# Token-set parts split when made and loaded straight into place, and a second place for raw gate and up weights, in a spectral-plus-gated kernel

## The chip, the cores and the metric

One core of one Trainium2 chip. The metric is device microseconds for one execution of the kernel. The program uses TensorE (PE, with its weight loads PEld), VectorE (DVE), ScalarE (ACT), GpSimd (POOL, here mostly issuing DMAs) and SyncE (SP, which issues the other DMAs). The engines run side by side and meet at semaphores; each works through its own instructions in order.

## The reference

```python
def reference(A_x, A_dft_seq_re, A_dft_seq_im, A_dft_hid_re, A_dft_hid_im, B_x, B_W_gate, B_W_up, B_W_down):
    xn = _layernorm(A_x, axis=-1)                 # x is [1, 2048, 640]
    # _A_ref: Re(DFT_seq(DFT_hid(xn)))
    a = jnp.einsum("bsd,ed->bse", xn, dft_hid_re)
    b = jnp.einsum("bsd,ed->bse", xn, dft_hid_im)
    y = jnp.einsum("ts,bse->bte", dft_seq_re, a) - jnp.einsum("ts,bse->bte", dft_seq_im, b)
    # _B_ref: gated ReLU unit, F = 1728
    gate = jnp.einsum("bsd,df->bsf", xn, W_gate)
    up = jnp.einsum("bsd,df->bsf", xn, W_up)
    h = gate * (gate > 0) * up
    return A_x + y + jnp.einsum("bsf,fd->bsd", h, W_down)
```

All tensors are float32. The three gated weights are scaled by 64.

## The kernel before

**Products.** Every float32 operand is held as two parts, a high part (the value rounded for TensorE, copied by ACT in `split`, L123) and a low part (value minus high, a DVE subtraction, L124). A product is three matmuls, high by high, high by low, low by high (`mm3`, L129 to L131), each 128x128 by 128x512. The matrix products are arranged in the manner of Strassen, so sums and differences of blocks are made on DVE first.

**Phase 1: the sequence transform, up to about 404 us.** Four chunks of 512 output columns. The matrices come in blocks of 128x1024 (512 KB) by SP (`stream`, L593, loads at L599) into `raw` and `tk` tiles, DVE takes differences (L595), `split` writes both parts into one of three `cb` tiles, and PE uses them against the normalized tokens (`xs_late`, `xs_early`). A list of units (`todo`) is walked by `drive` (L677): each unit's load is issued four units ahead, its preparation two ahead, its matmuls now. Deferred work is put into the same walk at a later unit by `defer(units, f)`. `phase` (L697) writes the list from names: `T1` to `T4` and `B22` are blocks of the transform, `K` and `A` loads of token sets. Within phase 1 a scheduler then orders the instructions of each engine; in phase 2 PE, DVE and ACT keep the program's order.

**Token sets.** The gated unit works on two pairs of token blocks, 1024 tokens each. Each pair has nine blocks of 128x1024: B11 to B22, T1 to T4 and X4. For the first pair (index 1) they are made in phase 1 by `token_sets` (L320), in six steps put into the list nine units apart. A step loads raw rows and statistics into two `stage` tiles by POOL (L362, L363), makes normalized blocks (L368, L369) and differences (L375) on DVE six units later, and stores them to DRAM (`set1`) by POOL two units after that (L384): one block half in each of steps 0 and 1, four halves as two stores of 512 KB in each of steps 2 to 5. In the last chunk `load_set` (L661) brings each whole block back by SP to a `stage` tile (L669) and splits it with ACT and DVE into its place: the four T sets (`K`) into `r1`, the other five (`A`) into `xs_early`. The second pair's sets are made and brought back in phase 2 with the same functions.

**Phase 2: gate and up, after about 404 us.** `gate_up(n)` (L786) makes one unit of 128 gated features against the sets of a pair. `Weights` (L744) loads raw gate and up blocks to the tile `z` (SP, L750), makes sums on DVE (L756 to L760), and splits them into `gw` with ACT copies through L120 and subtractions (L770). The pool of `z` has one place; `Weights(n+2)` is created in `rest_ahead` of unit n. ACT also copies PSUM results (`p<-ps` and others, through L120). The remaining 64 features have a unit of their own (`gate_up_rest`, L858, rectifier L872). Phase 3 (`project`) does the hidden transform and the down projection.

Of the kernel before, what the change touches and what calls it, by code (L numbers as in the profile page):

```python
# [58 lines left out]
def fnet_reglu_kernel(  # L59
# [15 lines left out]
    nc = tc.nc  # L75
    keep = ctx.enter_context(tc.tile_pool(name="keep", bufs=1))
# [3 lines left out]
    dram_p = ctx.enter_context(tc.tile_pool(name="dram", bufs=1, space=bass.MemoryType.DRAM))  # L80
# [8 lines left out]
    xs_early = early_p.tile([P, D * S // P], F32R, name="xs_early")  # L89
# [1 line left out]
    eps_t = keep.tile([P, 1], F32, name="eps_t")  # L91
    stat = keep.tile([P, 2, NG, SG], F32, name="stat")
    rows = dram_p.tile([2, S], F32, name="rows")
    sets = [dram_p.tile([NSET, P, W2], F32, name=f"set{q}") for q in range(2)]

    firsts = [dram_p.tile([P, 3, CH], F32, name=f"first{c}") for c in range(NCHUNK)]
    pqd = [dram_p.tile([2, P, KD, CH], F32, name=f"pq{c}") for c in range(NCHUNK)]
# [18 lines left out]
    def stage():  # L116
        return stages[-1].tile([P, W2], F32, name="st")
# [4 lines left out]
    def split(hi, lo, src):  # L122
        nc.scalar.activation(hi, src, AF.Copy)  # L123
        return nc.vector.tensor_tensor(lo, src, hi.bitcast(F32), op=OP.subtract)  # L124
# [30 lines left out]
    ph1 = ExitStack()  # L155
# [2 lines left out]
    tk = ph1.enter_context(tc.tile_pool(name="tk", bufs=NH))  # L158
    sums = ph1.enter_context(tc.tile_pool(name="sums", bufs=1))
    small = ph1.enter_context(tc.tile_pool(name="small", bufs=2))  # L160
    late_p = ph1.enter_context(tc.tile_pool(name="late", bufs=1, side="right"))
    xs_late = late_p.tile([P, D * S // P], F32R, name="xs_late")

# [19 lines left out]
    late = {}  # L183
# [136 lines left out]
    def token_sets(q, step, stage=stage, unit=None):  # L320

        ch = xt[:, q * W2 : (q + 1) * W2].rearrange("(k p) t -> k p t", p=P)
        st_r = rows[:, q * W2 : (q + 1) * W2]
        tt = nc.vector.tensor_tensor
        part = lambda st, i: st[:, i * CH : (i + 1) * CH]
        t = {}

        def later(load, make, keep):
            def begin():
                load()  # L330
                for m in make:
                    defer(6, m)
                defer(8, keep)

            todo.append((begin, idle, idle, idle))

        unit = unit or later

        if step < 2:
            cs = slice(step * CH, (step + 1) * CH)  # L340

            def load():
                t["mr"], t["a"] = stage(), stage()[:, :CH]
                for i in range(2):
                    nc.gpsimd.dma_start(part(t["mr"], i), st_r[i : i + 1, cs].to_broadcast([P, CH]))
                nc.gpsimd.dma_start(t["a"], ch[4][:, cs])

            def make():
                tc.keep_in_program_order(tt(t["a"], t["a"], part(t["mr"], 0), op=OP.add))
                tt(t["a"], t["a"], part(t["mr"], 1), op=OP.mult)  # L350

            unit(load, [make], lambda: nc.gpsimd.dma_start(sets[q][X4][:, cs], t["a"]))
            return

        k, hs = (step - 2) // 2, (step - 2) % 2 * HC
        hs = slice(hs, hs + HC)
        cols = lambda ap: ap.rearrange("p (c t) -> p c t", c=2)

        def load():
            t["mr"], t["ab"] = stage(), stage()  # L360
            for i in range(2):
                nc.gpsimd.dma_start(cols(part(t["mr"], i)), cols(st_r[i : i + 1])[:, :, hs].to_broadcast([P, 2, HC]))  # L362
                nc.gpsimd.dma_start(cols(part(t["ab"], i)), cols(ch[k + 2 * i])[:, :, hs])  # L363

        def make():
            mr, ab = t["mr"], t["ab"]
            for i in range(2):
                tc.keep_in_program_order(tt(part(ab, i), part(ab, i), part(mr, 0), op=OP.add))  # L368
                tt(part(ab, i), part(ab, i), part(mr, 1), op=OP.mult)  # L369

        def more():

            mr, ab = t["mr"], t["ab"]
            (a0, a1, b0, b1), (t1, t2, t3, t4) = ([st[:, i * HC : (i + 1) * HC] for i in range(4)] for st in (ab, mr))
            sub = lambda o, i0, i1: tt(o, i0, i1, op=OP.subtract)  # L375
            sub(t1, a1, a0)
            sub(t2, b1, t1)
            sub(t3, b1, a1)
            sub(t4, b0, t2)

        def keep_sets():
            cs = slice(k * CH + hs.start, k * CH + hs.stop)
            for i, st in ((B11, t["ab"]), (T1, t["mr"])):
                nc.gpsimd.dma_start(sets[q][i : i + 4, :, cs].rearrange("i p t -> p i t"),  # L384
                                  st.rearrange("p (i t) -> p i t", i=4))

        unit(load, [make, more], keep_sets)

    def raw():
        return raw_p.tile([P, W2], F32, name="raw")  # L390
# [202 lines left out]
    def stream(c, name, g):  # L593
# [53 lines left out]

        todo.append((load, prepare, run, lambda: combine(c, name) if g == NH - 1 else None))

    def set_parts(q, i):  # L650
        if i in SETS_A:
            t, b = xs_early, (SETS_A_NEXT, SETS_A)[q].index(i) * 2 * W2
        else:
            t, b = late["sets_b"][q], SETS_B.index(i) * 2 * W2
        return t[:, b : b + W2], t[:, b + W2 : b + 2 * W2]

    def set_half(q, i, j):
        h, l = set_parts(q, i)
        return h[:, j * CH : (j + 1) * CH], l[:, j * CH : (j + 1) * CH]

    def load_set(q, blocks, get=stage):  # L661
        t = {}

        def load():
            if "sets_b" not in late:
                late["sets_b"] = {1: get_r1(F32R)}
            for i in blocks:
                t[i] = get()
                nc.sync.dma_start(t[i], sets[q][i])  # L669

        def prepare():
            for i in blocks:
                split(*set_parts(q, i), t[i])

        return load, prepare, idle, idle

    def drive(far, ahead):  # L677

# [18 lines left out]
    def phase(c, names):  # L697


        for n in names.split():  # L700
            if n == "K":
                todo.append(load_set(1, [first_sets.pop(0)]))
            elif n == "A":
                todo.append(load_set(1, [early_sets.pop(0)]))
            elif n[0] == "W":
                sums_124(int(n[1]))
            elif n[0] == "V":
                sums_3(int(n[1]))
            elif n[0] == "B" and n[2] == "1":
                first_stream(int(n[3]), n[:3], int(n[4]))  # L710
            else:
                stream(c, n[:-1], int(n[-1]))
            if n == "V3":
                free[0] = len(todo) + 2
            if free[0] is not None and len(todo) >= free[0] and steps:
                token_sets(*steps.pop(0))
                free[0] = len(todo) + SPACE
# [6 lines left out]
    for c in range(1, NCHUNK - 1):  # L724
        phase(c, "T10 T11 T12 T13 T20 B220 T21 B221 T22 T23 B222 B223 T30 T31 T32 T33 T40 T41 T42 T43")
    assert not steps, len(steps)
    phase(NCHUNK - 1, "T10 K T11 T12 K T13 T20 B220 K T21 B221 K T22 T23 B222 B223 T30 A T31 A T32 A T33 A T40 A T41 T42 T43")
    assert not early_sets and not first_sets
    drive(4, 2)
    ph1.close()  # L730


    ph2 = ExitStack()
    for n, b, side in (("prep", 2, "left"), ("z", 1, "left"), ("wr", 1, "left"), ("tmp", 1, "left"), ("hob", 2, "left"),
                       ("stage3", 2, "left"), ("sets", 1, "left"), ("gw1", 1, "right")):
        open_pools[n] = ph2.enter_context(tc.tile_pool(name=n, bufs=b, side=side, reuse_waits="tile"))
    pool = open_pools.__getitem__
# [48 lines left out]
    def gate_up(n):  # L786
# [110 lines left out]

    def next_set(i, n, since=1, get=stage3, soon=False):

        load, prepare, _, _ = load_set(0, [i], get)  # L900

        def first():
            if 0 not in late["sets_b"] and i in SETS_B:
                late["sets_b"][0] = pool("sets").tile([P, len(SETS_B) * 2 * W2], F32R, name="sets_b")
            load()

        loads[n - since].append(first)
        (urgent if soon else besides)[n].append(prepare)

    def pair_weights(k, n):  # L910

# [338 lines left out]
```

## Time and profile before

| | |
|---|---|
| Median of three timed runs | 1047.72 us (1043.9 to 1048.57) |
| Profiled execution, first to last instruction (span) | 1043.3 us; no other time of this execution is recorded |
| Mean granted TensorE clock in it | 0.997 |
| TensorE busy | 1028.4 us |
| VectorE busy | 802.1 us |
| ScalarE busy | 433.5 us |
| GpSimd busy | 95.7 us |
| DMA | 233.29 MB, mean 224 GB/s |

How to read what follows. The windows view gives, for each stretch, the busy time of every engine with its number of instructions, the granted clock (1.00 is full), the DMA share and GB/s. The waits view lists, for an engine, which group waited for which, the total, the number and the longest. The chain follows the work that ended last backwards; a row is start, length, what. The timeline's rows are start, length, engine, line, operation, output and input, count, and in brackets the idle time ahead with what released it. Buffer numbers are left out of names, so `st` is any `stage` tile and `cb` any of three. Successive matmuls overlap, so their pitch is read from their starts.

### The profile page before, as it was taken

The numbers are of one execution on the slowest core, as the hardware profiler recorded it, in microseconds if no ns is written. First come the engines' busy times: TensorE is split into PE (matmuls) and PEld (weight loads), VectorE is DVE, ScalarE is ACT, GpSimd is POOL, SyncE is SP. The second block draws the span as 40 slices with busy tenths as digits, with TensorE's granted clock in tenths as the row PEclk, the third lists the DMA queues.
The fourth block names the chain that finished last, engine by engine and source line by source line (L and its number), as shares of the span: only waits on it lengthen the run. The fifth ranks groups of instructions, "written<-read, shape, count | busy, mean of one in ns | idle before, by whom it ended". The sixth has DMA issues, their size and how long they took to land.

```text
span 1043.3 us, 12416 instructions
## 1 busy us (share of the span) xinstructions
PE 1028.4 (99%) x4528; PEld 847.3 (81%) x4528; DVE 802.1 (77%) x1071; ACT 433.5 (42%) x543; POOL 95.7 (9%) x156
## 2 busy tenths in 40 slices
PE   8999999999999899899999999999999999999998
PEld 7888888888887788688888888888888888888886
DVE  7857886978979887577887988887488667786764
ACT  6654453333333443333334534343355423552521
POOL 2000010101211001421110000100000000000000
PEclk9999999999999999999999999999999999999999
DMA  7985754958867863863364566565498637986454
GB/s 294 340 247 170 261 161 140 311 205 269 305 199 259 339 203 116 251 222 143 131 206 177 203 224 232 215 237 188 145 393 287 207 111 218 366 300 233 157 159 121
DMA packets 100156, 233.29 MB, mean 224 GB/s; under 512 B 11392, under 2 KB 50816, under 8 KB 98688
## 3 DMA queue, kind: packets, MB, share of 16 engines
q1 hardware_dynamic: 83664, 166.96, 47.6%
q0 software_dynamic: 16432, 65.55, 17.4%
q8 instruction: 35, 0.57, 0.2%
q14 instruction: 25, 0.20, 0.1%
HBM read 177.41 MB, written 54.02 MB: 222 GB/s over the span
## 4 chain that ended last, share of the span: by engine, by line
PE 84%; DMA 5%; DVE 5%; issue 4%; ACT 2%; POOL 0%; SPq 0%; ACTq 0%; POOLq 0%; DVEq 0%
PE ps L131 27%; PE ps L130 27%; PE ps L129 27%; DMA z<-in_wgu 2%; DVE cb L124 1%; DMA r<-in_x 1%; DMA st<-set 1%; PE ps L1147 1%; PE ps L483 1%; ACT cb L123 1%; DMA set<-st 1%; DMA rw<-hd 1%; DVE raw L595 0%; DVE gw L770 0%; ACT gw L120 0%
## 5 line engine op out<-in xcount | busy, mean ns | idle before, releaser
L131 PE MATMUL ps<-cb,wt 128*128 128x512 f32 x390 | 151.9, 390 | 0.1
L129 PE MATMUL ps<-cb,wt 128*128 128x512 f32 x390 | 151.8, 389 | 0.0
L130 PE MATMUL ps<-cb,wt 128*128 128x512 f32 x390 | 151.7, 389 | 0.0
L124 DVE TENSOR_TENSOR cb<-rw,cb 128x1024 fp32r<-128x1024 f32 x83 | 94.2, 1135 | 66.6 <-ACT cb L123 65.9
L123 ACT ACTIVATE cb<-rw 128x1024 fp32r<-128x1024 f32 x83 | 81.9, 987 | 145.2 <-PE ps L131 125.0
L123 ACT ACTIVATE cb<-raw 128x1024 fp32r<-128x1024 f32 x78 | 82.5, 1059 | 124.9 <-PE ps L131 108.3
L124 DVE TENSOR_TENSOR cb<-raw,cb 128x1024 fp32r<-128x1024 f32 x78 | 95.1, 1221 | 41.2 <-ACT cb L123 38.0
L130 PE MATMUL ps<-xs_early,gw 128*128 128x512 f32 x260 | 101.2, 389 | 0.0
L129 PE MATMUL ps<-xs_early,gw 128*128 128x512 f32 x260 | 101.2, 389 | 0.0
L131 PE MATMUL ps<-xs_early,gw 128*128 128x512 f32 x260 | 101.1, 389 | 0.0
L130 PE MATMUL ps<-cb,xs_late 128*128 128x512 f32 x256 | 99.8, 390 | 0.9 <-DVE cb L124 0.8
L131 PE MATMUL ps<-cb,xs_late 128*128 128x512 f32 x256 | 99.7, 389 | 0.3 <-DVE xs_late L251 0.3
L129 PE MATMUL ps<-cb,xs_late 128*128 128x512 f32 x256 | 99.6, 390 | 0.4 <-ACT cb L123 0.4
L130 PE MATMUL ps<-cb,xs_early 128*128 128x512 f32 x238 | 92.8, 390 | 1.5 <-DVE cb L124 1.5
L129 PE MATMUL ps<-cb,xs_early 128*128 128x512 f32 x238 | 92.6, 391 | 1.1 <-ACT cb L123 1.1
L120 ACT ACTIVATE gw<-z 128x1024 fp32r<-128x1024 f32 (+1 forms) x52 | 57.8, 1111 | 84.2 <-DVE z L760 68.7
L131 PE MATMUL ps<-cb,xs_early 128*128 128x512 f32 x238 | 92.1, 389 | 0.0
L131 PEld LDWEIGHTS ps<-cb,wt 128*128 128x128 f32 x390 | 73.2, 188 | 15.7 <-DVE wt L124 0.5
L130 PEld LDWEIGHTS ps<-cb,wt 128*128 128x128 f32 x390 | 73.2, 188 | 15.4
L129 PEld LDWEIGHTS ps<-cb,wt 128*128 128x128 f32 x390 | 73.2, 188 | 15.2
L120 ACT ACTIVATE u<-ps 128x512 f32<-128x512 f32 x52 | 31.2, 599 | 93.0 <-PE ps L131 93.0
L770 DVE TENSOR_TENSOR gw<-z,gw 128x1024 fp32r<-128x1024 f32 (+1 forms) x52 | 64.8, 1286 | 2.3 <-ACT gw L120 2.2
(192 smaller groups left out, 1932.1 us busy)
## 6 DMA issues: line engine op xcount, KB each, us to landing
raw<-in_dft SPq DMA_DIRECT2D x94, 512.0 KB, 5.7
wt<-wparts SPq DMA_DIRECT2D x66, 256.0 KB, 3.2
z<-in_wgu SPq DMA_DIRECT2D x26, 640.0 KB, 4.0
hd<-ob POOLq DMA_DIRECT2D x26, 512.0 KB, 3.5
rw<-hd SPq DMA_DIRECT2D x24, 512.0 KB, 6.1
wparts<-pw POOLq DMA_DIRECT2D x11, 1024.0 KB, 4.1
tk<-in_dft SPq DMA_DIRECT2D x16, 512.0 KB, 6.2
rw<-pq SPq DMA_DIRECT2D x16, 512.0 KB, 7.7
```

The source lines that it names most:

```text
L120: return nc.scalar.activation(o, i, AF.Copy)
L123: nc.scalar.activation(hi, src, AF.Copy)
L124: return nc.vector.tensor_tensor(lo, src, hi.bitcast(F32), op=OP.subtract)
L129: nc.tensor.matmul(ps, wh, mh, start=first, stop=False, skip_group_check=more)
L130: nc.tensor.matmul(ps, wh, ml, start=False, stop=False, skip_group_check=more)
L131: nc.tensor.matmul(ps, wl, mh, start=False, stop=last, skip_group_check=more)
L483: nc.tensor.matmul(E[c, key], xn_part(j, d)[v == 1], b[c][0][:, int(v == 2), j], start=j == 0 and v == 0, stop=False)
L770: tt(self.w[:, 1, cs], self.z[:, cs], self.w[:, 0, cs].bitcast(F32), op=OP.subtract)
L1147: nc.tensor.matmul(B[key], wr[:, v, es], hr[:, cs], start=False, stop=v == 1, skip_group_check=not new)
```

## The change

Three parts. (1) The first pair's sets become `halves`, with a high and a low part of each block in DRAM. In each of its steps, `halve` splits a finished tile: the high part by ACT to a new tile `hi` (a pool of one place, shared by both tiles of a step), the low part by DVE in place of the block; `keep` stores the two parts by POOL. The first tile of a step is split six units after the loads and stored one later, the second two units after the first. (2) In the last chunk `load_halves` brings both parts of a block by one SP DMA of 1 MB straight to their place, with no stage tile and no split; the `K` loads stand later in the list, the `A` loads begin earlier. (3) The pool of `z` has two places, `Weights(n+2)` is created at the beginning of `gate_up(n)`, and the pools of phase 2 are opened in another order. In the new file the sources of `split` are at L124 and L125, matmuls at L130 to L132, DFT loads at L617 and their differences at L613, high and low stores at L399 and L400, `load_halves` at L687.

```diff
-    sets = [dram_p.tile([NSET, P, W2], F32, name=f"set{q}") for q in range(2)]
+    sets = dram_p.tile([NSET, P, W2], F32, name="set0")
+    halves = dram_p.tile([NSET, P, 2, W2], F32, name="set1")
...
+    high_p = ph1.enter_context(tc.tile_pool(name="high", bufs=1))
...
-        def later(load, make, keep):
-            def begin():
-                load()
-                for m in make:
-                    defer(6, m)
-                defer(8, keep)
-
-            todo.append((begin, idle, idle, idle))
...
+            made = [([make, more], "ab", lambda v: halves[B11 : B11 + 4, :, v, cs].rearrange("i p t -> p i t"), by_set),
+                    ([], "mr", lambda v: halves[T1 : T1 + 4, :, v, cs].rearrange("i p t -> p i t"), by_set)]
...
+        def begin():
+            load()
+            for i, (make, name, place, view) in enumerate(made):
+
+                def halve(make=make, name=name):
+                    for m in make:
+                        m()
+                    src = t[name]
+                    if "h" not in t:
+                        t["h"] = high_p.tile([P, W2], F32R, name="hi")
+                    split(t["h"][:, : src.shape[1]], src.bitcast(F32R), src)
+
+                def keep(name=name, place=place, view=view):
+                    src = t[name]
+                    nc.gpsimd.dma_start(place(0), view(t["h"][:, : src.shape[1]].bitcast(F32)))
+                    nc.gpsimd.dma_start(place(1), view(src))
+
+                defer(6 + 2 * i, halve)
+                defer(7 + 2 * i, keep)
+
+        todo.append((begin, idle, idle, idle))
...
-    def load_set(q, blocks, get=stage):
-        t = {}
+    def load_halves(i):
 
         def load():
             if "sets_b" not in late:
                 late["sets_b"] = {1: get_r1(F32R)}
-            for i in blocks:
-                t[i] = get()
-                nc.sync.dma_start(t[i], sets[q][i])
-
-        def prepare():
-            for i in blocks:
-                split(*set_parts(q, i), t[i])
-
-        return load, prepare, idle, idle
+            t, b = set_place(1, i)
+            nc.sync.dma_start(t[:, b : b + 2 * W2].bitcast(F32), halves[i].rearrange("p v t -> p (v t)"))
+
+        todo.append((load, idle, idle, idle))
...
-    phase(NCHUNK - 1, "T10 K T11 T12 K T13 T20 B220 K T21 B221 K T22 T23 B222 B223 T30 A T31 A T32 A T33 A T40 A T41 T42 T43")
+    phase(NCHUNK - 1, "T10 T11 T12 T13 T20 K B220 K T21 K B221 K T22 A T23 A B222 B223 T30 A T31 A T32 A T33 T40 T41 T42 T43")
...
-    for n, b, side in (("prep", 2, "left"), ("z", 1, "left"), ("wr", 1, "left"), ("tmp", 1, "left"), ("hob", 2, "left"),
+    for n, b, side in (("prep", 2, "left"), ("tmp", 1, "left"), ("wr", 1, "left"), ("hob", 2, "left"), ("z", 2, "left"),
                        ("stage3", 2, "left"), ("sets", 1, "left"), ("gw1", 1, "right")):
...
+        if n + 2 < NU:
+            weights[n + 2] = Weights(n + 2)
         for f in issues[n]:
             f()
...
-            if n + 2 < NU:
-                weights[n + 2] = Weights(n + 2)
             for f in loads[n]:
                 f()
```

The second pair keeps whole blocks: it takes the same functions through `unit`, `keep_whole` and `next_set`, which now has the load and the split written out.

More of the change, by code (lines that the diff above doesn't have):

```diff
@@ L326, in token_sets @@
         t = {}
-        def later(load, make, keep):
-            def begin():
-                load()
-                for m in make:
-                    defer(6, m)
-                defer(8, keep)
-            todo.append((begin, idle, idle, idle))
-        unit = unit or later
         if step < 2:
@@ L350, in make @@
                 tt(t["a"], t["a"], part(t["mr"], 1), op=OP.mult)
-            unit(load, [make], lambda: nc.gpsimd.dma_start(sets[q][X4][:, cs], t["a"]))
-            return
[L355 to L387, printed above, removed]
+            made = [([make], "a", lambda v: halves[X4][:, v, cs], lambda ap: ap)]
+            keep_whole = lambda: nc.gpsimd.dma_start(sets[X4][:, cs], t["a"])
+        else:
+            k, hs = (step - 2) // 2, (step - 2) % 2 * HC
+            hs = slice(hs, hs + HC)
+            cols = lambda ap: ap.rearrange("p (c t) -> p c t", c=2)
+            cs = slice(k * CH + hs.start, k * CH + hs.stop)
+            def load():
+                t["mr"], t["ab"] = stage(), stage()
+                for i in range(2):
+                    nc.gpsimd.dma_start(cols(part(t["mr"], i)), cols(st_r[i : i + 1])[:, :, hs].to_broadcast([P, 2, HC]))
+                    nc.gpsimd.dma_start(cols(part(t["ab"], i)), cols(ch[k + 2 * i])[:, :, hs])
+            def make():
+                mr, ab = t["mr"], t["ab"]
+                for i in range(2):
+                    tc.keep_in_program_order(tt(part(ab, i), part(ab, i), part(mr, 0), op=OP.add))
+                    tt(part(ab, i), part(ab, i), part(mr, 1), op=OP.mult)
+            def more():
+                mr, ab = t["mr"], t["ab"]
+                (a0, a1, b0, b1), (t1, t2, t3, t4) = ([st[:, i * HC : (i + 1) * HC] for i in range(4)] for st in (ab, mr))
+                sub = lambda o, i0, i1: tt(o, i0, i1, op=OP.subtract)
+                sub(t1, a1, a0)
+                sub(t2, b1, t1)
+                sub(t3, b1, a1)
+                sub(t4, b0, t2)
+            by_set = lambda ap: ap.rearrange("p (i t) -> p i t", i=4)
+            made = [([make, more], "ab", lambda v: halves[B11 : B11 + 4, :, v, cs].rearrange("i p t -> p i t"), by_set),
+                    ([], "mr", lambda v: halves[T1 : T1 + 4, :, v, cs].rearrange("i p t -> p i t"), by_set)]
+            def keep_whole():
+                for i, st in ((B11, t["ab"]), (T1, t["mr"])):
+                    nc.gpsimd.dma_start(sets[i : i + 4, :, cs].rearrange("i p t -> p i t"), by_set(st))
@@ new lines, in token_sets @@
+        if unit:
+            unit(load, made[0][0], keep_whole)
+            return
+        def begin():
[14 more added lines that the diff above has]
+                defer(7 + 2 * i, keep)
@@ L648, in stream, with set_place @@
         todo.append((load, prepare, run, lambda: combine(c, name) if g == NH - 1 else None))
+    def set_place(q, i):
+        if i in SETS_A:
+            return xs_early, (SETS_A_NEXT, SETS_A)[q].index(i) * 2 * W2
+        return late["sets_b"][q], SETS_B.index(i) * 2 * W2
     def set_parts(q, i):
[L651 to L654, printed above, removed]
+        t, b = set_place(q, i)
         return t[:, b : b + W2], t[:, b + W2 : b + 2 * W2]
@@ L701, in phase @@
             if n == "K":
-                todo.append(load_set(1, [first_sets.pop(0)]))
+                load_halves(first_sets.pop(0))
             elif n == "A":
-                todo.append(load_set(1, [early_sets.pop(0)]))
+                load_halves(early_sets.pop(0))
             elif n[0] == "W":
@@ L898, in next_set, with load @@
     def next_set(i, n, since=1, get=stage3, soon=False):
-        load, prepare, _, _ = load_set(0, [i], get)
-        def first():
+        t = {}
+        def load():
             if 0 not in late["sets_b"] and i in SETS_B:
                 late["sets_b"][0] = pool("sets").tile([P, len(SETS_B) * 2 * W2], F32R, name="sets_b")
-            load()
-        loads[n - since].append(first)
-        (urgent if soon else besides)[n].append(prepare)
+            t["st"] = get()
+            nc.sync.dma_start(t["st"], sets[i])
+        loads[n - since].append(load)
+        (urgent if soon else besides)[n].append(lambda: split(*set_parts(0, i), t["st"]))
     def pair_weights(k, n):
```

## The prediction

> **What bounds the kernel now.** I read the page's busy times first, then the table of 20 us windows over the stretches the change touches, then the waits there, and last the chain and the timeline around each loss.
>
> ```profile
> span 1043.3 us, 12416 instructions
> PE 1028.4 (99%) x4528; PEld 847.3 (81%) x4528; DVE 802.1 (77%) x1071; ACT 433.5 (42%) x543; POOL 95.7 (9%) x156
> 220.00:240.00 20.00, 20.00 (x90) 16.57 (x89) 15.18 (x18) 7.22 (x9) 3.48 (x5) 1.00 0.42 150
> 260.00:280.00 20.00, 19.87 (x87) 15.98 (x86) 20.00 (x25) 6.38 (x6) 5.53 (x8) 1.00 0.95 328
> 280.00:300.00 20.00, 20.00 (x90) 16.56 (x89) 13.67 (x17) 7.57 (x8) 2.30 (x4) 1.00 0.67 242
> 320.00:340.00 20.00, 18.84 (x82) 15.03 (x81) 18.18 (x20) 6.22 (x7) 1.86 (x3) 1.00 0.90 292
> 340.00:360.00 20.00, 17.36 (x73) 13.33 (x72) 15.85 (x16) 9.16 (x11) 0.54 (x1) 1.00 0.96 374
> 420.00:440.00 20.00, 16.33 (x66) 13.09 (x65) 11.99 (x20) 7.32 (x10) 7.64 (x11) 0.92 0.78 251
> ```
>
> PE sets the end: it is busy 99% of the span, and an undisturbed 20 us holds 90 matmuls, 0.222 us each. The change leaves the matmuls alone, so only PE's stalls count. The columns after the window's length are PE, PEld, DVE, ACT and POOL, the granted clock, the DMA share and GB/s. Two losses stand out. Between 320 and 360 us there are 82 + 73 matmuls instead of 180: 25 x 0.222 = 5.5 us. Between 420 and 440 there are 66: 24 x 0.222 = 5.3 us, part of it at a lower granted clock. Between 260 and 280 DVE is busy all of the time and PE loses 0.5 us; there is no room there. In the other two rows DVE has 4.8 and 6.3 us to spare.
>
> The first loss, in the waits of that stretch, in the chain, and on ACT:
>
> ```profile
> ACT r L123 <- DMA st<-set: 15.0, 3, 5.4
> PE ps L130 <- DVE cb L124: 2.3, 3, 0.8
> PE ps L129 <- ACT cb L123: 1.5, 2, 1.1
> ...
> 322.80 7.12 DMA set<-st
> 330.13 0.33 SPq L669
> 332.32 9.33 DMA st<-set
> ...
> 341.67 1.06 ACT L123 ACTIVATE r<-st 128x1024 fp32r<-128x1024 f32 x1 [5.11 <-DMA st<-set]
> 342.64 1.04 ACT L123 ACTIVATE cb<-tk 128x1024 fp32r<-128x1024 f32 x1
> ```
>
> SP stands at the first set load until the last set store lands (322.80 + 7.12), then issues a burst; a set block takes 9.33 us to land; ACT waits for it three times, 15.0 us in all, with the next high part of a DFT block queued behind (342.64 after 341.67). PE waits for those parts.
>
> The second loss:
>
> ```profile
> 405.11 24.05 SPq L750 DMA_DIRECT2D z<-in_wgu  x3
> ...
> 428.83 6.37 DMA z<-in_wgu
> ...
> 435.29 1.06 ACT L120 ACTIVATE gw<-z 128x1024 fp32r<-128x1024 f32 x1 [6.88 <-DMA z<-in_wgu]
> 436.25 0.58 ACT L120 ACTIVATE p<-ps 128x512 f32<-128x512 f32 x1
> ...
> 432.82 0.39 PE L131 MATMUL ps<-xs_early,gw 128*128 128x512 f32 x1
> 436.88 0.79 PE L129 MATMUL ps<-r,gw 128*128 128x512 f32 x1 [3.67 <-ACT p L120]
> 440.29 0.40 PE L131 MATMUL ps<-r,gw 128*128 128x512 f32 x1
> ```
>
> There is one place for raw gate and up weights, so the third load starts only at 428.83, when unit 1's weights are used up. ACT waits 6.88 us for it ahead of the copy that PE needs. PE starts nothing from 432.82 to 436.88 (4.06, less one pitch of 0.23: 3.8 us); then the eight starts up to 440.29 take 3.41 us instead of 8 x 0.227 = 1.8 (half clock), another 1.6. Together 5.4 us.
>
> **The change part by part.** (1) Second raw place. Unit 2's weights are requested at the beginning of unit 0, about 10 us before 428.83, once unit 0's are used; the first two loads no longer wait for each other either. The 6.88 us wait is covered and 5.4 us go. What is late next is only the steady order of the later units, where no stall stands in the trace. The moved pools put the small stage of phase 2 over the tile of the last spectral store, so the rectifier after the first rest product waits for that store's landing:
>
> ```profile
> 409.76 0.53 POOL L568 DMA_DIRECT2D pq<-sa  x1 [7.17 <-DVE sa L493]
> 414.57 0.59 ACT L872 ACTIVATE st<-ps 64x512 f32<-64x512 f32 x1
> ```
>
> 409.76 plus a landing of 4 to 5 us is about 414.57: taken at 0; a 7.1 us landing (below) would be 2.3 us late on ACT, and PE has other banks to fill meanwhile.
>
> (2) Last chunk. Nine ACT splits and their nine DVE subtractions leave, so the three ACT waits and PE's stalls of 320 to 360 go: 5.5 us. The set loads, now 1 MB straight into place, wait for the last store as before, and one load of the rest weights has been scheduled ahead of six DFT loads and waits for a store as well. What it delays are the same DFT loads that the first set load delays now, and these no longer share the burst with three set blocks; I take nothing back, and 5.5 us if that cover is gone (a rival). Parts of the first pair are read only in the second phase, so a late 1 MB load costs nothing.
>
> (3) The splits move into the six token steps. Steps 2 to 5 each add two ACT copies, two DVE subtractions in place, and two more stores on POOL; counts over the whole kernel stay level, and 9.4 MB of DMA come on top of 233. The two high parts of a step share one tile, so the second ACT copy waits until the first one's store has landed, with the next DFT high part queued behind it on ACT, and the second subtraction (with DFT work behind it on DVE) waits for that copy. Landings:
>
> ```profile
> L123 ACT ACTIVATE cb<-raw 128x1024 fp32r<-128x1024 f32 x78 | 82.5, 1059 | 124.9 <-PE ps L131 108.3
> DMA to landing us min/median/max: 3.1/3.9/7.1
> DMA to landing us min/median/max: 2.3/4.2/10.1
> set<-st POOLq DMA_DIRECT2D x8, 512.0 KB, 4.7
> ```
>
> The first landing row is the store line L384, the second every DMA on a set. A subtraction takes 1.14 us from start to start (rows below: 325.66 - 322.25 = 3.41 for three). Steps 0 and 1 are half as large, and steps 2 and 4 lie in the windows with 4.8 and 6.3 us of spare DVE time, over two subtractions of 2.3: taken at 0, up to 1 us each if the landing is late.
>
> Step 3 has no cover:
>
> ```profile
> 259.52 0.69 DVE L369 TENSOR_TENSOR st<-st 128x512 f32<-128x512 f32 x1
> 263.74 1.28 DVE L493 TENSOR_TENSOR sa<-ps,sa 128x512 f32<-128x512 f32 x2
> 264.93 1.29 DVE L496 SCALAR_TENSOR_TENSOR sb<-sb,sa 128x512 f32<-128x512 f32 x2
> 266.13 1.22 DVE L595 TENSOR_TENSOR raw<-raw,tk 128x1024 f32<-128x1024 f32 x1
> 269.54 1.23 DVE L124 TENSOR_TENSOR cb<-raw,cb 128x1024 fp32r<-128x1024 f32 x1
> ...
> 269.28 0.62 PE L129 MATMUL ps<-cb,xs_late 128*128 128x512 f32 x2
> 270.82 0.50 PE L130 MATMUL ps<-cb,xs_late 128*128 128x512 f32 x1
> ```
>
> The source is ready at 260.2 (259.52 + 0.69), the first copy ends at 261.3, its store is issued about 261.7. The built order on DVE is: first subtraction, the two sa, second subtraction, then the two sb (264.93 now) and all that leads to the low part of 269.54, for which PE waits at 270.82. With a landing of L us the second copy ends at 261.7 + L + 1.06 and the subtraction 1.14 later, so the sb and PE come 261.7 + L + 2.2 - 264.93 = L - 1.0 us late, at least 2.3 (two subtractions, no wait; DVE being full, nothing below that). L = 3.9 gives 2.9 and 7.1 gives 6.1. Here the DMA share is 0.95, so I take the middle, L = 5.5: **4.5 us**.
>
> Step 5:
>
> ```profile
> 317.45 0.69 DVE L369 TENSOR_TENSOR st<-st 128x512 f32<-128x512 f32 x1
> 322.25 3.50 DVE L595 TENSOR_TENSOR raw<-raw,tk 128x1024 f32<-128x1024 f32 x3
> 325.66 2.36 DVE L124 TENSOR_TENSOR cb<-raw,cb 128x1024 fp32r<-128x1024 f32 x2
> ...
> 326.93 0.39 PE L129 MATMUL ps<-cb,xs_late 128*128 128x512 f32 x1
> ```
>
> The low part that starts at 325.66 ends just as PE takes it at 326.93: again no lead. First copy 318.1 to 319.2, store 319.6; second copy, second subtraction and one of the three L595 then stand ahead of it: 319.6 + L + 1.06 + 2 x 1.14 - 325.66 = L - 2.7 us late, at least 1.1 (two subtractions more, one L595 fewer). L = 3.9 gives 1.2, 7.1 gives 4.4. The page's median for these stores, 4.7, gives **2.0 us**.
>
> Sum: -5.4 - 5.5 + 4.5 + 2.0 = **-4.4 us**. The profiled span of 1043.3 becomes 1038.9. The median of the runs, 1047.72, lies 4.4 above that span (the lowest run, 1043.9, lies 0.6 above); I subtract from the median: **1043.3 us**.
>
> **A rule weighed.** After PE's idle 3.67 us the matmul pitch was 0.43 us. In step 3 the first high part also comes late (its L595 ends near 272 instead of 267.3, the copy near 273.1), so PE would stand from about 269.4 to 273.1, 3.7 us, in which the clock could halve as at 436.88, at the 1.6 us worked out there. [...]
>
> **The rivals.**
> A. The stores land in time (the minimum 3.1, or ACT gets to the second copy late anyway): only DVE's own work is left, 2.3 + 1.1 us: -10.9 + 3.4 = -7.5, **1040.2**. For it: the median landing of 3.9. Against: the DMA share of 0.95 and 0.90 in just these stretches, with twice the stores.
> B. Slower: the stores queue. Four per step now go through POOL, the DMA share is 0.9 already, and a set DMA took 10.1 us once. With L = 10.1 in both steps the stalls are 9.1 + 7.4, plus 1.6 for the clock in each: 19.7, against 10.9 gained: +8.8, **1056.5**. The price passes the gain at 2L - 3.7 = 10.9, so from L = 7.3 without the clock, 5.7 with both.
> C. The stall before 360 us stays, since SP still stands behind the last store and the DFT loads land in the same burst: -4.4 + 5.5 = +1.1, **1048.8**. For it: SP's 7.12 us. Against: ACT's queue, not DFT data, is what the waits name.
> D. The forecast, with the clock halved once near 273: -4.4 + 1.6 = -2.8, **1044.9**.
> E. It doesn't do what it says, neither place being free earlier: against it stands the built program's order, in which both loads come forward; under 0.02, within C.
>
> **How the numbers follow.** Forecast 0.43, A 0.21, B 0.16, C 0.10, D 0.10. A measurement of this kernel tells about 0.5%, 5.2 us, from no change. Faster by more: A, and the 0.16 of the forecast that its own spread (L from 3.9 to 7.1, -6.8 to -0.4, and some 2 us of the median's own scatter) puts below -5.2: 0.37. Slower by more: 0.14 of B. Same: 0.49. The range goes from 1038 (A less that scatter) to 1051 (C with its scatter); most of B and a tail of A stay outside, 0.2.
>
> **What would show it.** Right: a DVE and ACT wait on the landing of the hi store near 267 us, a PE gap of 4 to 5 us ending near 275 and one near 329; no ACT wait on a set DMA after 330; 88 to 90 matmuls in each 20 us up to 360 and again around 430, at granted clock 1.00. Wrong: a gap on z weights still there (1); PE waits for DFT blocks in the last chunk with SP at a store's landing (C); landings over 7 us (B); no PE gap at 270 (A).

## The result

The changed kernel takes 1052.88 us (median of four runs, 1048.9 to 1055.18) against 1046.98 us for the one before (median of four runs, one more than above, 1043.9 to 1048.57): ratio 1.0052, 95% interval 1.0029 to 1.0074. It is slower, by about 6 us, where 4.4 us less was forecast. Its profiled execution has a span of 1047.1 us (1043.3 before) and took 1048.9 us, the least of the four; the other three had spans of 1050.9 to 1053.4 us at a mean granted clock of 0.992 to 0.993 (0.995 in the profiled one).

The head of the changed kernel's page:

```profile
span 1047.1 us, 12457 instructions
PE 1028.8 (98%) x4528; PEld 848.1 (81%) x4528; DVE 802.6 (77%) x1072; ACT 432.9 (41%) x544; POOL 103.1 (10%) x166
```

Its windows, columns as before:

```profile
260.00:280.00 20.00, 13.11 (x48) 9.61 (x48) 18.64 (x24) 6.25 (x6) 4.17 (x6) 0.89 0.83 305
280.00:300.00 20.00, 20.00 (x84) 16.38 (x84) 15.83 (x20) 7.23 (x8) 3.65 (x6) 0.93 0.78 274
320.00:340.00 20.00, 18.66 (x83) 15.14 (x82) 18.27 (x23) 7.42 (x8) 3.38 (x5) 1.00 0.83 282
340.00:360.00 20.00, 19.21 (x86) 15.55 (x85) 18.20 (x19) 7.21 (x7) 2.61 (x4) 1.00 0.85 310
360.00:380.00 20.00, 18.25 (x81) 14.80 (x80) 9.89 (x9) 6.50 (x7) 0.00 (x0) 1.00 1.01 421
420.00:440.00 20.00, 20.00 (x89) 16.54 (x89) 11.17 (x18) 8.19 (x11) 7.96 (x13) 1.00 0.83 233
```

Around 430 us PE has 89 matmuls in 20 us at full clock: the weight stall is gone, as forecast. Between 260 and 280 it has 48 where the old kernel had 87, and the clock is down to 0.89 there and to 0.93 in the next window. The stall of the last chunk has thinned out from two windows over three.

The table that follows takes the successive starts of matmuls in a stretch that lie more than 0.25 us apart and sums what exceeds the pitch of 0.227 us. It is what PE lost there, idle time and half clock together, in the one profiled execution of each kernel. Ratios are against runs of the old kernel on the same chip (medians 1047.0 to 1047.9); for the kernel with whole rows and the second high tile, one of these, 1862.07 us at a granted clock of 0.727, is left out as slow.

| kernel | median us | ratio to before (95%) | 250 to 300 us | 300 to 400 us | 400 to 500 us |
|---|---|---|---|---|---|
| before | 1046.98 | | 0.5 | 5.4 | 5.4 |
| changed | 1052.88 | 1.0052 (1.0029 to 1.0074) | 10.5 | 4.7 | 0 |
| second place alone | 1038.61 | 0.9925 (0.9902 to 0.9948) | 0.5 | 7.9 | 0 |
| parts alone | 1056.77 | 1.0093 (1.0066 to 1.0119) | 11.0 | 5.2 | 8.1 |
| spacing ten | 1040.41 | 0.9931 (0.9911 to 0.9951) | 2.7 | 3.5 | 0 |
| steps three later | 1055.42 | 1.0075 (1.0059 to 1.0091) | 11.4 | 11.0 | 0 |
| halves one unit apart | 1051.96 | 1.0039 (1.0022 to 1.0056) | 11.3 | 9.3 | 0 |
| second high tile | 1053.16 | 1.0057 (1.0036 to 1.0078) | 9.0 | 10.2 | 0.1 |
| high stores from ScalarE | 1044.20 | 0.9973 (0.9958 to 0.9987) | 6.2 | 3.8 | 0 |
| whole-row stores | 1042.83 | 0.9956 (0.9936 to 0.9977) | 6.6 | 1.9 | 0 |
| whole rows, second high tile | 1038.91 | 0.9922 (0.9908 to 0.9937) | 2.8 | 2.3 | 0 |
| spacing ten, late sets | 1038.95 | 0.9916 (0.9902 to 0.9930) | 2.5 | 3.3 | 0 |
| set list alone | 1042.21 | 0.9952 (0.9936 to 0.9968) | 0.5 | 0 | 10.1 |
| second place and set list | 1034.46 | 0.9876 (0.9859 to 0.9893) | 0.5 | 0 | 0 |

**Where the 10.5 us come from.** GpSimd, VectorE, ScalarE and TensorE of the changed kernel from token step 2 to step 3, from the timeline:

```profile
232.20 0.76 POOL L399 DMA_DIRECT2D set<-hi  x1 [21.58 <-ACT hi L124]
235.91 0.76 POOL L400 DMA_DIRECT2D set<-st  x1 [2.94 <-issue]
239.37 0.75 POOL L399 DMA_DIRECT2D set<-hi  x1 [2.70 <-issue]
244.56 0.76 POOL L400 DMA_DIRECT2D set<-st  x1 [4.44 <-DVE raw L613]
245.32 0.71 POOL L354 DMA_DIRECT2D st<-rows  x1
250.98 0.73 POOL L354 DMA_DIRECT2D st<-rows  x1 [4.95 <-issue]
251.71 1.45 POOL L355 DMA_DIRECT2D st<-in_xt  x2
...
236.75 1.23 DVE L125 TENSOR_TENSOR st<-st,hi 128x1024 fp32r<-128x1024 f32 x1 [0.78 <-ACT hi L124]
259.40 0.69 DVE L360 TENSOR_TENSOR st<-st 128x512 f32<-128x512 f32 x1 [4.27 <-DMA st<-in_xt]
...
270.39 1.06 ACT L124 ACTIVATE hi<-st 128x1024 fp32r<-128x1024 f32 x1 [4.16 <-DVE sa L511]
...
263.62 0.50 PE L131 MATMUL ps<-cb,xs_late 128*128 128x512 f32 x1 [2.51 <-DVE cb L125]
276.25 1.22 PE L130 MATMUL ps<-cb,xs_late 128*128 128x512 f32 x2 [4.38 <-ACT cb L124]
278.83 0.63 PE L131 MATMUL ps<-cb,xs_late 128*128 128x512 f32 x1
279.26 0.63 PE L132 MATMUL ps<-cb,xs_late 128*128 128x512 f32 x1
```

The four stores of step 2 go out at 232.2, 235.9, 239.4 and 244.6. The last one's data are ready at 238.0 (236.75 + 1.23), yet it leaves at 244.56; in the trace's record of landings (235.6, 239.1, 244.3, 250.7) each store leaves 0.3 us after the one before has landed. One load of rows follows the last store at once (245.32); the second leaves only 0.3 us after that store's landing (250.98). The raw tokens of step 3 are requested at 251.7, some 11 us later than in the old kernel:

```profile
239.49 0.72 POOL L363 DMA_DIRECT2D st<-in_xt  x1
241.00 0.73 POOL L363 DMA_DIRECT2D st<-in_xt  x1 [0.79 <-issue]
```

VectorE then stands 4.27 us for them at 259.40, with the transform's differences queued behind, and PE loses 2.8 us at 263.62. The step's chain is 4.0 us late from there (the first high copy starts at 264.20 where 260.2 was worked out), its second high copy waits for the landing of the first one's store on top (265.72 to 270.24 in the landings, though the label names VectorE), and PE loses 4.5 us up to 276.25. Behind that the starts are 0.43 to 0.59 us apart until 282.7, where the trace grants half the clock (0.50 from 275.77 to 282.60): 3.2 us more. 2.8 + 4.5 + 3.2 = 10.5.

### The profile page after: what moved, and what is told of

The parts are those of the page before. It is cut to its first block, busy times and chain, and to the rows that moved or that the text cites. A ratio compares the mean times of both kernels' runs of the same rounds, so it can differ in the third digit from the quotient of the medians.

```text
span 1047.1 us, 12457 instructions
## 1 busy us (share of the span) xinstructions
PE 1028.8 (98%) x4528; PEld 848.1 (81%) x4528; DVE 802.6 (77%) x1072; ACT 432.9 (41%) x544; POOL 103.1 (10%) x166
## 4 chain that ended last, share of the span: by engine, by line
PE 85%; issue 6%; DMA 4%; DVE 3%; POOL 1%; ACT 1%; SPq 0%; ACTq 0%; DVEq 0%; POOLq 0%
PE ps L130 28%; PE ps L131 28%; PE ps L132 28%; PE ps L1162 1%; PE ps L501 1%; DMA raw<-in_dft 1%; DMA set<-st 1%; DMA set<-hi 1%; DMA tk<-in_dft 1%; DVE cb L125 1%; DMA rw<-hd 1%; ACT cb L124 1%; DVE tk L613 0%; PE ps L473 0%; DVE raw L613 0%
## 5 line engine op out<-in xcount | busy, mean ns | idle before, releaser
L132 PE MATMUL ps<-cb,wt 128*128 128x512 f32 x390 | 151.9, 390 | 0.4 <-DVE wt L125 0.4
L130 PE MATMUL ps<-cb,wt 128*128 128x512 f32 x390 | 151.8, 389 | 0.0
L125 DVE TENSOR_TENSOR cb<-rw,cb 128x1024 fp32r<-128x1024 f32 x83 | 94.1, 1133 | 69.7 <-ACT cb L124 67.8
L124 ACT ACTIVATE cb<-rw 128x1024 fp32r<-128x1024 f32 x83 | 81.9, 987 | 149.4 <-PE ps L132 122.8
L124 ACT ACTIVATE cb<-raw 128x1024 fp32r<-128x1024 f32 x78 | 82.5, 1059 | 125.5 <-PE ps L132 108.0
L125 DVE TENSOR_TENSOR cb<-raw,cb 128x1024 fp32r<-128x1024 f32 x78 | 95.2, 1220 | 39.3 <-ACT cb L124 36.0
L130 PE MATMUL ps<-cb,xs_late 128*128 128x512 f32 x256 | 100.2, 393 | 4.4 <-ACT cb L124 4.4
L132 PE MATMUL ps<-xs_early,gw 128*128 128x512 f32 x260 | 101.1, 389 | 0.0
L130 PE MATMUL ps<-xs_early,gw 128*128 128x512 f32 x260 | 101.1, 389 | 0.0
L132 PE MATMUL ps<-cb,xs_late 128*128 128x512 f32 x256 | 100.4, 392 | 0.0
L130 PE MATMUL ps<-cb,xs_early 128*128 128x512 f32 x238 | 93.2, 393 | 0.8 <-ACT cb L124 0.8
L132 PE MATMUL ps<-cb,xs_early 128*128 128x512 f32 x238 | 92.1, 389 | 0.0
L132 PEld LDWEIGHTS ps<-cb,wt 128*128 128x128 f32 x390 | 73.2, 188 | 15.9 <-DVE wt L125 0.7
L130 PEld LDWEIGHTS ps<-cb,wt 128*128 128x128 f32 x390 | 73.2, 188 | 15.2
```

The costliest lines, as they stand in the source:

```text
L130: nc.tensor.matmul(ps, wh, mh, start=first, stop=False, skip_group_check=more)
L132: nc.tensor.matmul(ps, wl, mh, start=False, stop=last, skip_group_check=more)
```

## The experiments

Theory S: a step with four stores outlasts its nine units, so the next step's loads are late. Rival H: the loss is only the second high copy's wait for the first one's store. Rival P: it is the place, since step 3 meets the stretch in which VectorE has no time left. Theory Q, formed after the first eight runs, says why the step is long.

**Second place alone.** The old kernel with `("z", 2, "left")`, the new order of the pools and `Weights(n + 2)` at the beginning of `gate_up(n)`.

> The second place for raw weights alone, with the reordered pools and the earlier request; the token sets as before. Theory S (the loss lies in the token steps: with parts stored one after the other through one high tile a step outlasts its nine units, so the next step's loads come late) and theory H (it lies only in the second high copy's wait for the first one's store) both expect the 5.4 us of the stall around 432 us to go and nothing else: about 1041.5 us, ratio 0.995 to before. If this part cost something that the changed kernel's trace hides, the ratio would be 1 or more.

1038.61 us. The stall at 432 us goes and nothing appears in its place. The gain, 8.7 us, is larger than the 5.4 us of the old kernel's profiled execution; that stall isn't one size (8.1 us in the profiled run of the parts alone and 10.1 in that of the list alone, below). The stall of the last chunk stays; its 7.9 us come from the longest of the six executions (1042.95 us, the others 1038.4 to 1040.1).

**Parts alone.** The changed kernel with the old pools, one place and the late request.

> The parts split when made and loaded straight into place, with the one place for raw weights as before. If the two parts add up, the 5.9 us by which the changed kernel is slower plus the 5.4 us of the weight stall: about 1058 us, ratio 1.011, with the stall around 270 (about 10 us with the half clock) in the trace. If the two parts interfere, less than 1.008 or more than 1.014.

1056.77 us, 9 to 10 us slower than before; the stall at 270 us is there at 11.0 us. The loss is in this part: with the second place's gain of 8.7 us the two would make 0.7 us, where the changed kernel lost 5.9. The intervals overlap, so an effect of the two parts on each other is neither shown nor excluded.

**Spacing ten.**

```diff
-    SPACE = 9
+    SPACE = 10
```

> The changed kernel with ten units between token steps instead of nine. Theory S: the loads of the next step find their stage tile free, the wait of VectorE for them (4.3 us at 259 us) and PE's first gap there (2.7 us) go, and what is left of the step's stall is at most the 4.5 us predicted: about 1046 us, ratio 0.999. Theory H: the wait on the high tile is as before, so is the loss: about 1052 us, ratio 1.005.

1040.41 us, 12 us less than the changed kernel, more than S had asked. VectorE no longer waits for raw tokens, and no half clock is left (granted 1.00 in each 20 us from 240 to 300). H falls as the only cause, since ScalarE still waits for the first high store in step 3:

```profile
ACT hi L124 <- DMA set<-hi: 4.7, 1, 4.7
```

But ten units also move step 3.

**Steps three units later, spacing nine.**

```diff
-                free[0] = len(todo) + 2
+                free[0] = len(todo) + 5
```

> The changed kernel with all token steps three units later and the spacing still nine, so that step 3 stands where the spacing of ten put it. Theory S (the spacing is too short for the longer step): VectorE's wait for the step's raw loads stays at 4 us or more somewhere and with it a gap of PE and the half clock, about 1050 us, ratio 1.003. Theory P (it is only the place: step 3 meets the stretch at 260 us in which VectorE has no time left): it goes as with ten, about 1041 us, ratio 0.994.

1055.42 us. Step 3 stands where ten units had put it, and the wait for raw tokens is as long as ever:

```profile
271.25 0.69 DVE L360 TENSOR_TENSOR st<-st 128x512 f32<-128x512 f32 x1 [5.79 <-DMA st<-in_xt]
```

P falls; it is the spacing.

**Halves one unit apart.** `defer(6 + i, halve)` and `defer(7 + i, keep)` in place of `2 * i`.

> The changed kernel, spacing nine, with the second tile of a step split and stored one unit after the first, not two. Theory S: the last store of a step and with it the next loads come one unit (2.7 us) earlier, VectorE's wait of 4.3 us falls to about 1.6 and the first gap of PE goes; the wait on the high tile stays: about 1047 us, ratio 1.000. Theory P or H: step 3 has the same work in the same place and the same wait: about 1053 us, ratio 1.006.

1051.96 us: S had asked for 1047, and that missed. The edit did not do what it was meant to. The last store of step 2 leaves at 243.96 instead of 244.56 although its data are ready at 237.3, and the wait for raw tokens is 3.9 us:

```profile
238.63 0.75 POOL L399 DMA_DIRECT2D set<-hi  x1 [2.69 <-issue]
243.96 0.76 POOL L400 DMA_DIRECT2D set<-st  x1 [4.58 <-DVE raw L613]
...
258.32 0.69 DVE L360 TENSOR_TENSOR st<-st 128x512 f32<-128x512 f32 x1 [3.91 <-DMA st<-in_xt]
```

So it isn't the place in the list that sets when the stores go.

**Second high tile.** The second high part goes to a tile of the raw ring:

```diff
-                    if "h" not in t:
-                        t["h"] = high_p.tile([P, W2], F32R, name="hi")
-                    split(t["h"][:, : src.shape[1]], src.bitcast(F32R), src)
+                    if name == "mr":
+                        t["h" + name] = raw().bitcast(F32R)
+                    else:
+                        t["h" + name] = high_p.tile([P, W2], F32R, name="hi")
+                    split(t["h" + name][:, : src.shape[1]], src.bitcast(F32R), src)
...
```

> The changed kernel with the second high part of each step in a tile of the raw ring, so that it doesn't wait for the first one's store. Theory H: the gap of 4.5 us ending at 276 and the half clock behind it go, 7 to 8 us: about 1045 us, ratio 0.998. Theory S: the second store still comes two units after the first, only some 2 us earlier, so the late loads of the next step stay and with them the first gap and part of the second: about 1050 us, ratio 1.003; a raw tile that is held for a store may cost a further microsecond.

1053.16 us, no gain. ScalarE has no wait on a high store any more, but the four stores still go one by one and VectorE's wait for raw tokens is 6.1 us. H falls a second time, and S as it was put, too: the serial copies aren't what makes the step long.

**High stores from ScalarE.** Theory Q: GpSimd's DMA queue holds one of these stores at a time.

```diff
-                    nc.gpsimd.dma_start(place(0), view(t["h"][:, : src.shape[1]].bitcast(F32)))
+                    nc.scalar.dma_start(place(0), view(t["h"][:, : src.shape[1]].bitcast(F32)))
```

> The changed kernel with the stores of the high parts issued by ScalarE's DMA queue, right behind the copy, instead of GpSimd's; low parts as before. Theory Q: GpSimd's queue takes the next store of a step only when the one before has landed (in the changed kernel's trace each is issued 0.3 us after the landing of the one before), so four stores in place of two hold back the next step's loads. Then with two stores per step the loads come some 7 us earlier, VectorE's 4.3 us for raw rows and PE's first gap at 260 us go, and what stays is the wait on the high tile in step 3: about 1047 us, ratio 0.999. If the lateness comes from the order of the work on VectorE and not from that queue: about 1053 us, ratio 1.005.

1044.20 us, better than asked. The wait for raw tokens of step 3 is gone, and the loss before 300 us is 6.2 us.

**Whole-row stores.** The halves lie in DRAM as `[2, 4, P, 2, W2]`, so that a store writes 4 KB in one run per partition; the set loads gather by two DMAs a block:

```diff
+            for v in range(2):
+                nc.sync.dma_start(d[:, v * W2 : (v + 1) * W2].rearrange("p (s c) -> p s c", s=4),
+                                  halves[g, :, :, v, j * HC : (j + 1) * HC].rearrange("s p c -> p s c"))
```

> The changed kernel with another layout in DRAM: each store writes one run of 4 KB per partition (128 pieces) instead of four of 1 KB (512 pieces), and the set loads of the last chunk gather 1 KB pieces instead, two DMAs per block. If it is the number of pieces that makes GpSimd's queue hold one store at a time, the stores follow each other without waiting, the loads are in time, and the loss at 260 to 283 us falls from 10.5 us to 3 to 5: about 1047 us, ratio 0.999. If it is the bytes or the store itself: about 1053 us, ratio 1.005, or more where the gathers are slower.

1042.83 us. The same bytes in a quarter of the pieces, and the stores of step 2 follow their data without waiting for each other:

```profile
231.38 0.56 POOL L400 DMA_DIRECT2D set<-hi  x1 [21.47 <-ACT hi L125]
233.36 0.53 POOL L401 DMA_DIRECT2D set<-st  x1 [1.43 <-DVE st L126]
235.87 0.53 POOL L400 DMA_DIRECT2D set<-hi  x1 [1.97 <-ACT hi L125]
237.03 0.53 POOL L401 DMA_DIRECT2D set<-st  x1 [0.63 <-DVE st L126]
237.67 1.47 POOL L355 DMA_DIRECT2D st<-rows  x2
...
266.09 1.06 ACT L125 ACTIVATE hi<-st 128x1024 fp32r<-128x1024 f32 x1 [4.78 <-DMA set<-hi]
267.18 1.23 DVE L126 TENSOR_TENSOR st<-st,hi 128x1024 fp32r<-128x1024 f32 x1 [2.16 <-ACT hi L125]
```

Second and fourth store leave 2.0 and 1.2 us after the one before them, and none of these stores landed in less than 2.8 us. The rows for step 3 are requested at 237.67. This shows Q.

The number of pieces is what fits all runs. The record of each issue gives its pieces: 512 for a store in 1 KB pieces, 256 for one of these steps' loads of rows or tokens, 128 for a store in 4 KB pieces. Summed over GpSimd's DMAs that are issued and not yet landed, they come to 896 at most, in each of the fourteen traces, while the bytes reach 1.5 to 2 MB. Two stores of 512 pieces would be 1024, and wherever one directly follows another (twelve of the kernels), it leaves 0.30 to 0.37 us after the first has landed.

What stays in step 3 is the wait that the prediction had priced: ScalarE waits 4.78 us for the first store's landing, at 265.9 (267.2 was worked out).

**Whole rows and the second high tile.** Both edits together.

> Stores of whole rows as in the run of that name (1042.8 us, loss 6.6 us between 250 and 300 us), and the second high part of each step in a tile of the raw ring, so that it doesn't wait for the first one's landing (4.8 us on ScalarE in step 3). If what is left in step 3 is that wait and the half clock behind its idle time, the loss falls to the two subtractions, 2 to 3 us at full clock: about 1039 us, ratio 0.992. If it is VectorE's work alone, or if the borrowed raw tile holds the transform's loads instead: about 1043 us or more, ratio 0.996.

1038.91 us, 4 us less, and the loss before 300 us falls from 6.6 to 2.8 us with the clock at 1.00 in each 20 us from 240 to 300. So H is a part of the loss, seen only once the queue is out of the way; 2.8 is near the two subtractions of 2.3.

**Spacing ten and late sets.** The four K loads of the last chunk behind B222.

> Spacing ten, and the four K loads of the last chunk moved behind the B22 blocks, where the stores have long landed. If SyncE standing at the last store causes the rest of the stall between 340 and 360 us (3.5 us with spacing ten), about 1038 us, ratio 0.991. If the load of the rest weights, which waits for a store as well, holds SyncE alone, no change: 1040.4 us, ratio 0.993.

1038.95 us against 1040.41 of spacing ten, not measured side by side; the intervals of the ratios overlap, and the stall of the last chunk is 3.3 us instead of 3.5. The edit, which moves some of the A loads back too, did not get the K loads past the stores: the first leaves at 357.56, as the last store lands (357.54). So this settles nothing about SyncE's wait there.

**The list of the last chunk without the parts.** First with the second place, then alone; the sets are stored whole and split after loading, as before.

```diff
-"T10 K T11 T12 K T13 T20 B220 K T21 B221 K T22 T23 B222 B223 T30 A T31 A T32 A T33 A T40 A T41 T42 T43"
+"T10 T11 T12 T13 T20 K B220 K T21 K B221 K T22 A T23 A B222 B223 T30 A T31 A T32 A T33 T40 T41 T42 T43"
```

> The token sets whole and split in the last chunk as before, with the second place for raw weights and the list of the last chunk (places of K and A) of the changed kernel. If the stall before 360 us (5.4 us, with a half clock 7.9 in the run of the second place alone) comes from where the loads stand in the list, it goes to under 2 us: about 1034 us, ratio 0.987. If the splits behind a landing on ScalarE are the cause wherever they stand, it only moves: 1038.6 us or more, ratio 0.992.

> The kernel before with only the list of the last chunk (places of the K and A loads) of the changed kernel; sets whole and split there as before, one place for raw weights. With the second place this list left no stall before 400 us. If the two gains add up, the 5.4 us stall of 335 to 352 us goes and the weight stall at 432 us stays: about 1042 us, ratio 0.995.

1034.46 us with the second place, the fastest kernel here, ratio 0.9876 to before; 1042.21 us alone. All nine splits are still made, the two gains multiply (0.9925 x 0.9952 is 0.9877), and the stall of the last chunk is gone in both. Windows of the first of the two:

```profile
320.00:340.00 20.00, 20.00 (x90) 16.52 (x88) 19.45 (x20) 6.39 (x7) 2.10 (x4) 1.00 0.98 366
340.00:360.00 20.00, 20.00 (x90) 16.57 (x89) 16.90 (x15) 12.23 (x14) 0.29 (x1) 1.00 0.87 324
420.00:440.00 20.00, 20.00 (x90) 16.55 (x89) 16.77 (x28) 7.98 (x11) 8.74 (x14) 1.00 0.77 246
```

Its waits between 320 and 360 us (total, times, longest):

```profile
ACT r L123 <- DMA st<-set: 6.4, 3, 4.0
```

And SyncE's first set loads in its timeline:

```profile
331.49 0.82 SPq L669 DMA_DIRECT2D st<-set  x2
```

ScalarE still waits 6.4 us for set blocks (15.0 before), but the transform's blocks are ahead by then: the first set load leaves at 331.5 with the T1 loads ahead of it in SyncE's order, not behind.

## Why the prediction was wrong

**(1) The second raw place: right.** 5.4 us were to go at 432 us; the loss there is 0 in every kernel that has it.

**(2) The last chunk: wrong in its cause and its size.** The step read "Nine ACT splits and their nine DVE subtractions leave, so the three ACT waits and PE's stalls of 320 to 360 go: 5.5 us". The ACT waits on set blocks went, but 3.1 us of stalls came in their place (1.1 at 347 and 2.0 at 367 us). Ahead of the first, VectorE has no idle time from 335 to 350 us. The second of them in the changed kernel's timeline:

```profile
341.25 0.33 SPq L868 DMA_DIRECT2D st<-in_wrest  x1
...
345.60 0.48 SPq L617 DMA_DIRECT2D tk<-in_dft  x1
356.59 0.86 SPq L687 DMA_DIRECT2D r<-set  x2
...
368.70 0.50 PE L131 MATMUL ps<-cb,xs_early 128*128 128x512 f32 x1 [1.75 <-DVE cb L125]
```

The waits between 315 and 372 us and the chain have what lies between:

```profile
DVE tk L613 <- DMA raw<-in_dft: 7.4, 1, 7.4
```

```profile
357.54 8.72 DMA raw<-in_dft
```

SyncE stands twice: before the load of the rest weights, until a store lands at 341.1 (the prediction took this at nothing, and VectorE then waits only 0.6 us for a transform block), and from 346 to 356.6 before the first 1 MB load, whose last store left at 348.89 and landed at 356.45. The raw block behind it lands 8.72 us after its request, in the burst. That is rival C in part; with whole-row stores the last one lands at 339.5 and this second stall is not there. And the list alone removes the whole stall with the splits kept: what had to leave was the place of the loads, not the splits.

**(3) Step 3: wrong by 5.5 us.** The term was 4.5, the measured loss 10.5 against 0.5 before. The step that failed is "the source is ready at 260.2": it was taken from the old kernel, as if the loads of step 3 did not depend on the stores of step 2. They go into the same stage tiles and through the same queue, and "two more stores on POOL" were counted as bytes only. The old kernel's trace had it:

```profile
260.66 0.76 POOL L384 DMA_DIRECT2D set<-st  x1 [8.02 <-DVE st L375]
266.56 0.77 POOL L384 DMA_DIRECT2D set<-st  x1 [5.15 <-DVE sb L496]
```

The second store came 5.9 us after the first, 0.35 us after the first had landed (266.21), with a label that looked like a wait for data, and these 512 KB stores took 3.1 to 7.1 us to land. With that out of the way (whole rows) the chain is as worked out: landing 5.5 us (260.48 to 265.94), PE's gap 3.8 us. That the landing met the middle value taken is luck: the high stores of steps 2 to 5 took 2.9 to 8.0 us there. The half clock behind the gap, which was a rival at 1.6 us, came too, at 3.2 us in the changed kernel and 2.8 with whole rows (granted 0.83 from 260 to 280 us there).

**Step 5: right, some 10 us later than foreseen.** 2.0 us forecast, 1.6 measured (1.34 us idle at 338.58 and the slow start behind it), behind the wait that was named, with a landing of 4.5 us:

```profile
333.94 1.06 ACT L124 ACTIVATE hi<-st 128x1024 fp32r<-128x1024 f32 x1 [4.05 <-DMA set<-hi]
```

**The sum.** Step 3 came out 5.5 us dearer and the last chunk, step 5 included, 2.8 us (-0.7 in place of -3.5): 8.3 us, against 8.2 between the forecast span of 1038.9 and the measured 1047.1. Rival B came nearest: it had the sign, and said that the stores queue, four per step. But it priced this as landings of 10 us in two steps' own waits. No store of step 3 took longer than 8.2 us to land; it was their number, one behind the other, that held back the next step's loads. That the medians differ by 5.9 us and the profiled spans by 3.8 comes with a lower granted clock in the other three runs (0.992 to 0.993 against 0.995); where in them the clock fell isn't recorded.

**The half clock.** In the changed kernel the idle time of 4.4 us was followed by starts 0.43 us apart at a granted clock of 0.50; its other idle times near 260 us and in the last chunk, 2.5 us and less, were not. In the run of the second place alone the idle time was broken: PE started one matmul in 3.8 us (at 351.43, 2.56 us after the one before and 1.26 us ahead of the next), and by 353.28 the starts were 0.43 us apart (granted 0.91 over 340 to 360 us). In the run of the halves one unit apart the same spacing began at 264.09, behind a single gap of 2.5 us (260.00 to 262.54), so the length of one gap does not decide alone. What else does was not shown.

## What to carry to other kernels

When a change doubles the stores of a step, follow the queue that issues them to the next loads in it and into the same tiles, and not only the step's own waits; count the pieces that would be under way in it, not only the bytes. In short: a term that starts from an old start time is wrong if anything ahead of that start has changed. When a stall is a wait for a load, try first where in the list the load stands; here that alone removed the stall that the rebuilding of the data was meant to remove, with the splits kept. Test the parts of a change one by one: the fastest kernel here keeps two of them and leaves out the one that costs.

## What the runs showed of the hardware

GpSimd's queue issued a 512 KB store of 512 pieces of 1 KB only 0.3 us after the one before had landed (steps of 3.5 to 5.2 us in step 2), and stores of the same size in 128 pieces of 4 KB 1.2 to 2.5 us apart, before the one ahead had landed. In none of the fourteen traces were more than 896 pieces under way in it. The profile names such waits "issue" (2.94 us ahead of the second store of step 2 in the changed kernel) or the last work of another engine that happens to end near (4.44 us ahead of the fourth, put down to VectorE). ScalarE's queue took the two high stores of step 3 at 0.37 us each:

```profile
260.14 0.37 ACTq L399 DMA_DIRECT2D set<-hi  x1
```
